# Output columns dealt in turns of 32 to two halves, and three moved operations, in a chain of an FFT filter and two MLPs

## The chip, the cores and the metric

The kernel runs on one core of a Trainium2 chip. TensorE (PE) multiplies matrices, ACT, DVE and POOL work on whole tiles, SP issues most of the transfers, and 16 DMA engines carry them. The metric is the device time of one execution in microseconds (us). Three executions of the kernel before took 1126.7 us in the median (1125.58 to 1127.02).

## The reference

```python
X = np.fft.rfft(x, axis=1)                     # x: 2 x 3008 x 256, fp32
y = np.fft.irfft(X * (filt_r + 1j * filt_i), n=3008, axis=1)
x = y.reshape(6016, 256)
h = x @ w_in                                   # 256 -> 2048
x = (h / (1 + exp(-h))) @ w_out                # 2048 -> 256
g = x @ w_gate                                 # 256 -> 1536
v = x @ w_val
out = (g / (1 + exp(-g)) * v) @ w_out2         # 1536 -> 256, 6016 x 256 fp32
```

## The kernel before

Every matrix product is made from three products of operands split into a high and a low part. The program has an FFT stage (to some 125 us of the span), the first MLP with the preparation of all weights (to some 560 us), and the gated MLP. The change touches the preparation of w_out2 (key `o2`) and the gated MLP.

**The gated MLP.** The 6016 tokens go in six blocks t of 1024 (the last has 896), each of two token halves l. A block has six units (`Pair`, u = 6t + n, u from 0 to 35). A unit makes the gate g and the value v of a slice of the hidden width, by a scheme with seven products of half blocks (`Gate`: p15, p6, p3, p7, p4 and an `add` of product 2). Between its matmuls (`product`, L843) a queue feeds matmuls of the output products (`product7`, L1157): seven products k for each pair c of units, also by halves. In all a unit has 63 matmuls of 128x512, some 14.3 us, of which 21 are output products.

**What sets the order.** `run` (from L1013) writes a unit's steps down in order, with seven calls of `tick()` and calls `side(-1)` to `side(4)` between them. A tick advances the output products by one step: it splits a coming operand into high (`high7`, ACT L1104) and low (`lower7`, DVE L1109), adds finished products into the output tiles (`after7`, DVE L1130, ACT L1132), and issues weights (`load7`, SP L1118, tiles w7 from DRAM tensors d7). A side runs what a table (`later`, L1375 to L1396) puts there: `load_s2` (SP L648, weights wst from ds_g and ds_v for the next unit), x for the next block, and the stores of the block before. Each engine keeps its program's order, and a load can start only after SP has issued all that stands ahead of it.

**The gate's chain in a unit.** ACT computes silu of g.a (L1030) and of g.u2 (L1034). For u2, DVE first adds (L904, in p3). In p7 DVE adds c (L912). The value half starts with a copy of a bank by ACT (L876, `p15`) to which PE adds its products 6 and 7: PE waits for this copy. `join` (DVE L1011) ends the unit before. DVE's L1048 multiplies the value half a into silu of g.a.

**Stores.** Output products are by columns: half m of the 256 output columns, half l of the tokens. The sum for (t, m, l) ends in tile `oa`. `store2` (L1254) transposes one such part by 32x32 squares (DVE L1260) into a tile `ob` of pool tp, and SP sends it with four DMAs (L1265), one for each 32 partitions. They are held in `lag` until the next side. The output rows are 256 columns of fp32 in DRAM, and each DMA writes 32 columns, so its runs are of 128 bytes. For the last block, the last stores go from both SP and ACT at the end (`product8`).

**w_out2's preparation.** `load_w` loads raw weights, `comb_a` (POOL L516, L518) forms sums and differences of four quarters, `pieces` splits them into high (ACT L545, L550) and low (DVE L546 or POOL L551) and `store` sends them to d7 in DRAM.

**Pools.** Tiles of operands come from `mid`; those in the pool `late` (nine buffers: ga, w7, one ho) and `late2` (x and xo of the gated MLP) exist only in the gated MLP. SP's DMAs use eight semaphores in turn.

Of the kernel before, what the change touches and what calls it, by code (L numbers as in the profile page):

```python
# [29 lines left out]
P = 128  # L30
# [89 lines left out]
def fft_filter_mlp_kernel(  # L120
# [307 lines left out]
    def load_w(key, q, half):  # L428


        src = SRC[key]
        raw = mid([P, 512, 2], "raw", U32)
        raws[key, q, half] = raw
        if key == "o2":
            for j in range(2):
                r0 = 512 * q + 256 * half + P * j
                nc.sync.dma_start(
                    raw.rearrange("p (m j c) w -> p j m (c w)", m=2, j=2)[:, j],
                    src[r0:r0 + P, :].rearrange("p (m e) -> p m e", m=2),
                )  # L440
# [69 lines left out]

    def comb_a(key, q, part=None):
        v = pair[key, q] if key == "i1" else pair[key, q].bitcast(F32)
        if part != 1:
            sums[key, q] = mid([P, 4, 256], "ws")
        s = sums[key, q]
        sub = lambda o, a, b: nc.gpsimd.tensor_tensor(o, a, b, op=ALU.subtract)  # L516
        if part != 1:
            nc.gpsimd.tensor_tensor(s[:, 0], v[:, 0, 256:], v[:, 1, 256:], op=ALU.add)  # L518
            sub(s[:, 1], s[:, 0], v[:, 0, :256])
        if part != 0:  # L520
            sub(s[:, 2], v[:, 0, :256], v[:, 0, 256:])
            sub(s[:, 3], v[:, 1, :256], s[:, 1])
            if key == "i1":
                del pair[key, q]
# [14 lines left out]
    def pieces(q, keys, v):  # L539
        w = mid([P, len(keys), 2, 2, P], "wst", F32R)  # L540
        v = v.rearrange("p o (j c) -> p o j c", j=2)
        for n, k in enumerate(keys):
            o = w[:, n]
            if k in MINUS:
                nc.scalar.activation(o[:, :, 0], v[:, n], AF.Copy, scale=-1.0)  # L545
                nc.vector.scalar_tensor_tensor(  # L546
                    o[:, :, 1], v[:, n], -1.0, o[:, :, 0], op0=ALU.mult, op1=ALU.subtract
                )
            else:
                nc.scalar.copy(o[:, :, 0], v[:, n])  # L550
                nc.gpsimd.tensor_tensor(o[:, :, 1], v[:, n], o[:, :, 0], op=ALU.subtract)  # L551
        for n, k in enumerate(keys):
            store(d7[q][:, AT7.index(k)], w[:, n].rearrange("p j l c -> p (j l c)"))

    def comb_7(q, part):
        if part < 2:
            v = pair["o2", q].bitcast(F32)
            if part == 0:
                pieces(q, (1, 2), v[:, :, :256])
            else:  # L560
                pieces(q, (4,), v[:, 1:, 256:])
                if q == 2:
                    pieces(q, (8,), v[:, :1, 256:])
                del pair["o2", q]
        else:
            i = 2 * (part - 2)
            pieces(q, ((5, 6), (7, 3))[part - 2], sums["o2", q][:, i:i + 2])
            if i:
                del sums["o2", q]
# [413 lines left out]
    class Pair:  # L983
# [29 lines left out]
        def run(self, old, side):  # L1013
# [83 lines left out]
    def high7(c, k, p):  # L1097
        if (k, p) == (1, 0):
# [27 lines left out]
    def after7(c, k):  # L1126
# [8 lines left out]
        if (t, m) not in turned and k in (2, 3, 7, 4):  # L1135
            turned[t, m] = mid([P, 2, 512], "oa")
        o = turned[t, m][:, l, :n] if (t, m) in turned else None
# [62 lines left out]
    def product8(p, v, l, m, i):  # L1200
# [10 lines left out]
        if end and i == 2:  # L1211
            store2(t, m, l, (nc.sync, nc.scalar), o)

    def join8(m, l):
        t = NBLK2 - 1
        o = bank(4 + 2 * l + m)[:, :size2(t) // 2]
        nc.vector.tensor_tensor(o, o, turned[t, m][:, l, :o.shape[-1]], op=ALU.add)

    def tick():
# [27 lines left out]
        for r, o in enumerate((-3, 3, 9, 21)):  # L1247
# [6 lines left out]
    def store2(t, m, l, engines=(nc.sync,), src=None):  # L1254

        n = size2(t) // 2
        if src is None:
# [417 lines left out]
```

## Time and profile before

| | |
|---|---|
| median of three executions | 1126.7 us |
| profiled execution, own time | 1127.43 us |
| its span | 1125.7 us |
| PE busy | 1107.8 us, 98% |
| DVE, ACT, POOL busy | 75%, 69%, 35% |
| granted PE clock | 0.999 of full |
| output stores | 80 of 64 KB and 16 of 56 KB |

The span is what the profiler saw between the first and the last instruction of the profiled execution; 1.7 us lie around it. A time "at 745" is counted from the span's start. "Idle before" an instruction is what its engine waited, and the name behind the arrow is who ended the wait.

### The profile page before, as it was taken

How to read it: one execution, taken by the hardware profiler on the slowest of the kernel's cores; microseconds unless marked ns; L12 is line 12 of the kernel's file. 1: busy time of each engine (PE TensorE's matmuls, PEld its weight loads, DVE VectorE, ACT ScalarE, POOL GpSimd, SP SyncE). 2: the span in 40 equal slices, each digit the busy share in tenths (PEclk: the TensorE clock that was granted, in tenths of full speed). 3: DMA queues.
4: the chain of work that ended last, by engine and by line, in shares of the span. 5: the costliest groups of instructions: out<-in, count | busy, mean ns of one | idle time of the engine just before them, and what ended most of it. 6: DMA issues, size and time to landing. Idle time of an engine off the chain costs nothing.

```text
span 1125.7 us, 15425 instructions
## 1 busy us (share of the span) xinstructions
PE 1107.8 (98%) x4999; PEld 912.2 (81%) x4999; DVE 847.4 (75%) x1316; ACT 772.2 (69%) x1459; POOL 391.6 (35%) x369
## 2 busy tenths in 40 slices
PE   9999999999999999999999999999999999999997
PEld 7588888898888888788877778888888888778886
DVE  5888455567587687687665788898888888888877
ACT  5798766667677677666665676776676677677662
POOL 2667836454431362362101322322322322212220
PEclk9999999999999999999999999999999999999999
DMA  9974443435454445443747569898898898798895
GB/s 244 291 238 122 132 143 110 150 113 198 153 175 153 146 168 195 151 174 130 261 131 264 128 151 240 202 232 235 206 219 240 211 227 235 199 214 227 210 233 108
DMA packets 146977, 212.70 MB, mean 189 GB/s; under 512 B 58704, under 2 KB 88016, under 8 KB 146896
## 3 DMA queue, kind: packets, MB, share of 16 engines
q1 hardware_dynamic: 125280, 179.26, 50.0%
q0 software_dynamic: 17456, 31.79, 16.4%
q10 hardware_dynamic: 4160, 0.66, 0.3%
q8 instruction: 40, 0.66, 0.2%
q14 instruction: 41, 0.34, 0.1%
HBM read 138.20 MB, written 42.73 MB: 161 GB/s over the span
## 4 chain that ended last, share of the span: by engine, by line
PE 86%; DVE 6%; ACT 3%; DMA 2%; issue 2%; POOL 0%; SPq 0%; DVEq 0%; ACTq 0%
PE bk L843 25%; PE acc L742 15%; PE bk L1157 11%; PE acc L719 7%; PE h L669 6%; PE y L843 6%; PE xb L843 4%; PE xa L843 4%; PE s L206 2%; PE s L397 2%; PE s L209 2%; DMA wst<-ds_g 1%; PE s L282 1%; ACT ho L1104 1%; DVE ho L1109 1%
## 5 line engine op out<-in xcount | busy, mean ns | idle before, releaser
L742 PE MATMUL acc<-h,w 128*128 128x512 f32 x768 | 283.7, 389 | 0.0
L843 PE MATMUL bk<-xo,wst 128*128 128x512 f32 (+1 forms) x864 | 278.5, 387 | 5.1 <-ACT bk L876 2.9
L1157 PE MATMUL bk<-ho,w 128*128 128x512 f32 (+1 forms) x714 | 264.7, 387 | 0.9 <-DMA w<-d 0.9
L843 PE MATMUL bk<-xo,w 128*128 128x512 f32 (+1 forms) x648 | 208.9, 389 | 2.5 <-DVE c L912 1.9
L843 PEld LDWEIGHTS bk<-xo,wst 128*128 128x128 f32 x864 | 160.9, 188 | 42.1 <-ACT bk L876 7.9
L742 PEld LDWEIGHTS acc<-h,w 128*128 128x128 f32 x768 | 144.2, 188 | 29.6
L1091 POOL DMA_DIRECT2D ga<-c x68 | 59.6, 1100 | 308.6 <-DVE ho L1109 307.7
L1157 PEld LDWEIGHTS bk<-ho,w 128*128 128x128 f32 x714 | 133.9, 188 | 25.5 <-DMA w<-d 1.3
L843 PEld LDWEIGHTS bk<-xo,w 128*128 128x128 f32 x648 | 120.7, 188 | 31.7 <-DVE c L912 7.4
L1109 DVE TENSOR_TENSOR ho<-ga,ho 128x512 fp32r<-128x512 f32 (+1 forms) x136 | 95.2, 707 | 2.2 <-ACT ho L1104 2.2
L719 PE MATMUL acc<-h,w 128*128 128x512 f32 (+1 forms) x384 | 95.4, 376 | 0.0
L1104 ACT CAST ho<-ga 128x512 fp32r<-128x512 f32 (+1 forms) x136 | 82.8, 616 | 3.5 <-PE bk L843 2.7
L669 PE MATMUL h<-xh,w 128*128 128x512 f32 (+1 forms) x248 | 83.6, 379 | 0.1
L719 PEld LDWEIGHTS acc<-h,w 128*128 128x128 f32 x384 | 71.2, 188 | 11.2
L876 ACT COPY bk<-bk 128x512 f32<-128x512 f32 (+1 forms) x72 | 40.6, 565 | 54.2 <-PE bk L843 52.0
L677 DVE TENSOR_TENSOR h<-h,h 128x512 fp32r<-128x512 f32 (+1 forms) x64 | 41.4, 655 | 47.9 <-ACT h L676 46.5
L843 PE MATMUL xb<-xo,wst 128*128 128x512 f32 x192 | 74.7, 391 | 1.6 <-DVE h L939 1.6
L843 PE MATMUL xa<-xo,w 128*128 128x512 f32 x192 | 75.6, 395 | 0.0
L843 PE MATMUL y<-xo,wst 128*128 128x512 f32 x192 | 74.7, 389 | 0.0
L1109 DVE TENSOR_TENSOR ho<-c,ho 128x512 fp32r<-128x512 f32 (+1 forms) x102 | 72.6, 712 | 0.7 <-ACT ho L1104 0.6
L904 DVE TENSOR_TENSOR u<-bk,u 128x512 f32<-128x512 f32 (+1 forms) x72 | 48.7, 677 | 26.5 <-PE bk L843 23.3
L894 ACT COPY u<-bk 128x512 f32<-128x512 f32 (+1 forms) x72 | 41.9, 581 | 32.3 <-PE bk L843 26.9
(166 smaller groups left out, 2190.9 us busy)
## 6 DMA issues: line engine op xcount, KB each, us to landing
w<-d SPq DMA_DIRECT2D x53, 512.0 KB, 5.3
wst<-ds_g SPq DMA_DIRECT2D x36, 512.0 KB, 5.2
wst<-ds_v SPq DMA_DIRECT2D x36, 512.0 KB, 5.7
wst<-ds SPq DMA_DIRECT2D x32, 512.0 KB, 4.5
ga<-c POOLq DMA_DIRECT2D x60, 256.0 KB, 5.7
c<-ga POOLq DMA_DIRECT2D x30, 256.0 KB, 8.5
zt<-d SPq DMA_DIRECT2D x16, 384.0 KB, 5.4
d<-z SPq DMA_DIRECT2D x11, 512.0 KB, 4.3
```

What stands on the lines that cost most here:

```text
L669: nc.tensor.matmul(ps[:, :n], wt[key, f // 4, g][:, wpart, o:o + P], x[xpart][:, g, :n], start=(g == 0 and k == 0), stop=(g == 1 and k == 2),)
L677: nc.vector.tensor_tensor(h[:, 1, :n], u[:, :n], h[:, 0, :n], op=ALU.subtract)
L719: nc.tensor.matmul(a[:, :n], w[:, wpart, o:o + 128], h[:, xpart, :n], start=(f == 0 and k == 0), stop=(f == 15 and k == 2),)
L742: nc.tensor.matmul(a, w[:, wpart, o:o + 128], h[xpart][:, n * l:n * l + n], start=(f == 0 and k == 0), stop=(end and k == 1), skip_group_c ...
L843: nc.tensor.matmul(o, w(wpart), x[:, xpart, :o.shape[-1]], start=(first and k == 0), stop=(last and k == 2), skip_group_check=True,)
L876: nc.scalar.copy(self.y, self.a)
L894: nc.scalar.copy(self.u2, self.y)
L904: nc.vector.tensor_tensor(self.u2, self.b, self.u2, op=ALU.add)
L1091: nc.gpsimd.dma_start(o, v, accum_op=ALU.add)
L1104: nc.scalar.copy(x[:, 0, :v.shape[-1]], v)
L1109: nc.vector.tensor_tensor(x[:, 1, :n], v, x[:, 0, :n], op=ALU.subtract)
L1157: nc.tensor.matmul(o, w7[c, k][:, p, wpart], ops7[c, k, p][:, xpart, :n], start=(k in (1, 5) and p == 0 and i == 0), stop=(k in (2, 3, 4) ...
```

## The change

Output columns were halves 0 to 127 and 128 to 255. Now they are dealt in turns of 32: half m = 0 has columns 0 to 31, 64 to 95 and so on. To that end the quarters of w_out2 are read through strided views with runs of 32 (`turned_in`), in as many instructions as before, and w_out2 is loaded with one DMA for two. Two parts (m = 0 and 1) of one token half are transposed into one tile `ob` where a token's 64 neighbouring columns lie side by side, and four DMAs send it in runs of 256 bytes. So `turned` is keyed by token half, and the table of stores changes: transposes stand at (3,1) and (3,3) for l = 1 and both at (5,0) for l = 0, where there were four places with a group of stores each.

Besides, three operations move: the silu of g.u2 stands behind the next tick and p7 on ACT, DVE's L1048 stands behind its tick, and `load7` for r = 0 is issued one tick later. One more `ho` tile comes from pool `late`. Lines of the changed kernel are some 7 higher here (L1034 is L1043, L876 is L883, L648 is L655, L1118 is L1125), and the stores' 16 (L1265 is L1281).

```diff
 def load_w:  if key == "o2":
-            for j in range(2):
-                r0 = 512 * q + 256 * half + P * j
-                nc.sync.dma_start(...)
+            r0 = 512 * q + 256 * half
+            nc.sync.dma_start(
+                raw.rearrange("p (j f) w -> p j (f w)", j=2),
+                src[r0:r0 + 256, :].rearrange("(j p) f -> p j f", p=P),
+            )
...
+    def turned_in(v):
+        return v.rearrange("p o (x m c) -> p o m x c", m=2, c=32)
...
+        if key == "o2":
+            s, v = s.rearrange("p k (x c) -> p k x c", c=32), turned_in(v)
+            v00, v01, v10, v11 = (v[:, o, m] for o in range(2) for m in range(2))
...
             g.p3()
-            nc.scalar.activation(a[:, n:m], g.u2, AF.Silu)
             tick()
             g.p7()
+            nc.scalar.activation(a[:, n:m], g.u2, AF.Silu)
             side(1)
...
             v.add(v.a, 2, last=True)
+            tick()
             nc.vector.scalar_tensor_tensor(a[:, :n], v.a, -1.0, a[:, :n], op0=ALU.mult, op1=ALU.mult)
-            tick()
             v.p3()
...
-        if (k, p) == (1, 0):
+        if (k, p) in ((1, 0), (2, 0)):
             x = late["p"].tile([P, 2, 512], F32R, tag="mid", name="ho")
...
-        for r, o in enumerate((-3, 3, 9, 21)):
+        for r, o in enumerate((-2, 3, 9, 21)):
...
-    def store2(t, m, l, engines=(nc.sync,), src=None):
+    def store2(t, m, l, src=None, engines=(nc.sync,)):
         n = size2(t) // 2
+        if (t, l) not in outs:
+            if l and t < NBLK2 - 1:
+                outs[t, l] = late2["p"].tile([P, 16, 2, 32], F32, tag="x", name="ob", bufs=5)
+            else:
+                outs[t, l] = mid([P, 16, 2, 32], "ob")
+        o = outs[t, l]
         if src is None:
-            src = turned[t, m][:, l, :n]
-        o = tp.tile([P, 512], F32, tag="u", name="ob")
-        nc.vector.transpose(o[:, :n], src)
+            src = turned[t, l][:, m, :n]
+        nc.vector.transpose(o[:, :n // 32, m], src.rearrange("p (j c) -> p j c", c=32))
+        if m == 0:
+            return
...
-                    out[r0:r0 + n, P * m + 32 * i:P * m + 32 * i + 32].rearrange("(j r) c -> r j c", r=32),
-                    o[32 * i:32 * i + 32, :n].rearrange("p (j c) -> p j c", c=32),
+                    out[r0:r0 + n, 64 * i:64 * i + 64].rearrange("(j r) e -> r j e", r=32),
+                    o[32 * i:32 * i + 32, :n // 32].rearrange("p j m c -> p j (m c)"),
...
-        for n, k, m, l in ((3, 1, 0, 0), (3, 3, 0, 1), (4, 1, 1, 1), (5, 1, 1, 0)):
+        for n, k, m, l in ((3, 1, 0, 1), (3, 3, 1, 1), (5, 0, 0, 0), (5, 0, 1, 0)):
             later(6 * t + n, k, store2, t - 1, m, l)
```

The order on three engines, before and after.

On ACT in unit 3, from the silu of g.a to the copy that PE waits for (CAST is the high part of a coming operand, the first COPY is that of `after7`). Before:

```order
L1030 ACTIVATE ga_5885<-bk_5544 128x512
L1034 ACTIVATE ga_5885<-u2_5874 128x512
L1104 CAST ho_5892<-c_5678 128x512
L1132 COPY bk_5895<-bk_5868 128x512
L1104 CAST ho_5909<-ga_5791 128x512
L1104 CAST ho_5911<-c_5753 128x512
L876 COPY bk_5618<-bk_5543 128x512
```

After:

```order
L1037 ACTIVATE ga_5879<-bk_5538 128x512
L1111 CAST ho_5885<-c_5672 128x512
L1139 COPY bk_5888<-bk_5862 128x512
L1043 ACTIVATE ga_5879<-u2_5868 128x512
L1111 CAST ho_5903<-ga_5785 128x512
L1111 CAST ho_5905<-c_5747 128x512
L883 COPY bk_5612<-bk_5537 128x512
```

One cast and one copy that stood behind the silu of u2 now stand ahead of it.

On DVE at the boundary of blocks 1 and 2 (unit 11), from `join` on. Before:

```order
L1011 TENSOR_TENSOR c_6891<-bk_5543,c_6820 128x512
L1109 TENSOR_TENSOR ho_6915<-c_6352,ho_6915 128x512
L904 TENSOR_TENSOR u2_6925<-bk_5618,u2_6925 128x512
L1109 TENSOR_TENSOR ho_6929<-c_6480,ho_6929 128x512
L912 TENSOR_TENSOR c_6955<-bk_5542,s5_6909 128x512
L1260 STREAM_TRANSPOSE ob_6959<-oa_6187 128x512
```

After:

```order
L1018 TENSOR_TENSOR c_6874<-bk_5537,c_6806 128x512
L1274 STREAM_TRANSPOSE ob_6912<-oa_5998 128x16x32 x2
L1116 TENSOR_TENSOR ho_6898<-c_6346,ho_6898 128x512
L911 TENSOR_TENSOR u2_6909<-bk_5612,u2_6909 128x512
L1116 TENSOR_TENSOR ho_6916<-c_6474,ho_6916 128x512
L919 TENSOR_TENSOR c_6941<-bk_5536,s5_6892 128x512
```

The transpose behind the sum for c is now two transposes, behind `join` and ahead of the sum for u2.

On SP in block 4, from the load ds_g_98 for unit 28 to ds_v_100 for unit 30 (the number after ds_g or ds_v tells the six of a block, 94 to 99 and 100 to 105; w are the w7 tiles). Before:

```order
L648 DMA wst<-ds_g_98 128x1024
L1265 DMA out_dram<-ob 32x16x32 x4
L648 DMA wst<-ds_v_104 128x1024
L1118 DMA w_9165<-d_2_111 128x512
L1265 DMA out_dram<-ob 32x16x32 x4
L1118 DMA w_9207<-d_0_109 128x1024
L1118 DMA w_9242<-d_1_110 128x1024
L648 DMA wst<-ds_g_99 128x1024
L1265 DMA out_dram<-ob 32x16x32 x4
L648 DMA wst<-ds_v_105 128x1024
L1118 DMA w_9359<-d_1_110 128x1024
L648 DMA wst<-ds_g_94 128x1024
```

After:

```order
L655 DMA wst<-ds_g_98 128x1024
L655 DMA wst<-ds_v_104 128x1024
L1125 DMA w_9123<-d_2_111 128x512
L1281 DMA out_dram<-ob 32x16x64 x4
L1125 DMA w_9166<-d_0_109 128x1024
L655 DMA wst<-ds_g_99 128x1024
L1125 DMA w_9215<-d_1_110 128x1024
L655 DMA wst<-ds_v_105 128x1024
L1125 DMA w_9316<-d_1_110 128x1024
L1281 DMA out_dram<-ob 32x16x64 x4
L655 DMA wst<-ds_g_94 128x1024
L655 DMA wst<-ds_v_100 128x1024
```

Between the loads ds_g_98 and ds_g_99 stood two groups of stores and three w7 loads; now there are one group and two w7 loads. The group behind ds_g_99 is gone, and a group stands ahead of ds_g_94, where before one followed it (below the rows shown).

## Rows read from the trace of the kernel before

**Rows 1.** The page, part 1: busy us, share of the span, instructions of each engine.

```profile
PE 1107.8 (98%) x4999; PEld 912.2 (81%) x4999; DVE 847.4 (75%) x1316; ACT 772.2 (69%) x1459; POOL 391.6 (35%) x369
```

**Rows 2.** Busy time by stretch: PE, PEld, DVE, ACT, POOL (instructions), clock, DMA share, GB/s.

```profile
1000.00:1100.00 100.00, 96.98 (x452) 84.03 (x450) 82.71 (x141) 67.80 (x137) 23.65 (x27) 1.00 0.90 221
```

**Rows 3.** Waits of PE: line, releaser, total us, times, longest us.

```profile
PE bk L843 <- ACT bk L876: 2.9, 7, 1.3
PE bk L843 <- DMA wst<-ds_g: 2.1, 2, 1.2
PE bk L843 <- DVE c L912: 1.9, 3, 1.0
PE xb L843 <- DVE h L939: 1.6, 2, 1.0
```

**Rows 4.** PE in order of time: start, length, line, shape, [idle before, releaser].

```profile
632.99 0.84 PE L843 MATMUL bk<-xo,w 128*128 128x512 f32 x3
635.18 0.50 PE L843 MATMUL bk<-xo,wst 128*128 128x512 f32 x1 [1.34 <-ACT bk L876]
...
663.47 0.74 PE L843 MATMUL bk<-xo,wst 128*128 128x512 f32 x2 [0.28 <-ACT bk L876]
...
750.46 0.74 PE L843 MATMUL bk<-xo,wst 128*128 128x512 f32 x2 [0.28 <-ACT bk L876]
...
755.62 0.39 PE L843 MATMUL bk<-xo,wst 128*128 128x512 f32 x1
```

**Rows 5.** ACT in order of time, unit 3 and block boundary at 745 us.

```profile
631.95 0.63 ACT L1034 ACTIVATE ga<-u 128x512 f32<-128x512 f32 x1 [0.88 <-DVE u L904]
...
634.55 0.57 ACT L876 COPY bk<-bk 128x512 f32<-128x512 f32 x1
...
746.71 0.63 ACT L1034 ACTIVATE ga<-u 128x512 f32<-128x512 f32 x1 [1.10 <-DVE u L904]
```

**Rows 6.** DVE in order of time at the same boundary.

```profile
744.62 0.68 DVE L1011 TENSOR_TENSOR c<-bk,c 128x512 f32<-128x512 f32 x1
745.22 0.68 DVE L1109 TENSOR_TENSOR ho<-c,ho 128x512 fp32r<-128x512 f32 x1
745.98 0.69 DVE L904 TENSOR_TENSOR u<-bk,u 128x512 f32<-128x512 f32 x1
```

**Rows 7.** DVE transposes grouped by shape: count, busy us, mean ns, idle before.

```profile
L1260 DVE STREAM_TRANSPOSE ob<-oa 128x512 f32<-128x512 f32 x20 | 14.0, 699 | 0.0
```

**Rows 8.** SP issuing in order of time, five stretches: start, length, line, count.

```profile
748.52 3.67 SPq L1265 DMA_DIRECT2D out_dram<-ob  x4
...
986.61 6.09 SPq L1265 DMA_DIRECT2D out_dram<-ob  x4
...
996.77 0.37 SPq L648 DMA_DIRECT2D wst<-ds_g  x1
...
1098.10 6.04 SPq L1118 DMA_DIRECT2D w<-d  x3
...
1117.45 4.43 SPq L1265 DMA_DIRECT2D out_dram<-ob  x8
```

**Rows 9.** PE in order of time, late: the matmuls behind three waits.

```profile
1004.49 0.47 PE L843 MATMUL bk<-xo,wst 128*128 128x512 f32 x1 [1.17 <-DMA wst<-ds_g]
...
1087.34 0.44 PE L843 MATMUL bk<-xo,wst 128*128 128x448 f32 x1 [0.96 <-DMA wst<-ds_g]
...
1099.17 0.36 PE L1157 MATMUL bk<-ho,w 128*128 128x448 f32 x1
...
1104.67 0.47 PE L1157 MATMUL bk<-ho,w 128*128 128x448 f32 x1 [0.88 <-DMA w<-d]
```

**Rows 10.** Chain of waits, two of its longest pieces: start, us, what.

```profile
996.77 7.58 DMA wst<-ds_g
1080.36 6.85 DMA wst<-ds_g
```

**Rows 11.** Loads of line 648: from issue to landing.

```profile
DMA to landing us min/median/max: 3.1/5.3/8.8
```

More of the change, by code (lines that the diff above doesn't have):

```diff
@@ L515, in comb_a @@
         s = sums[key, q]
+        if key == "o2":
+            s, v = s.rearrange("p k (x c) -> p k x c", c=32), turned_in(v)
+            v00, v01, v10, v11 = (v[:, o, m] for o in range(2) for m in range(2))
+        else:
+            v00, v01, v10, v11 = (v[:, o, m:m + 256] for o in range(2) for m in (0, 256))
         sub = lambda o, a, b: nc.gpsimd.tensor_tensor(o, a, b, op=ALU.subtract)
         if part != 1:
-            nc.gpsimd.tensor_tensor(s[:, 0], v[:, 0, 256:], v[:, 1, 256:], op=ALU.add)
-            sub(s[:, 1], s[:, 0], v[:, 0, :256])
+            nc.gpsimd.tensor_tensor(s[:, 0], v01, v11, op=ALU.add)
+            sub(s[:, 1], s[:, 0], v00)
         if part != 0:
-            sub(s[:, 2], v[:, 0, :256], v[:, 0, 256:])
-            sub(s[:, 3], v[:, 1, :256], s[:, 1])
+            sub(s[:, 2], v00, v01)
+            sub(s[:, 3], v10, s[:, 1])
             if key == "i1":
@@ L540, in pieces @@
         w = mid([P, len(keys), 2, 2, P], "wst", F32R)
-        v = v.rearrange("p o (j c) -> p o j c", j=2)
         for n, k in enumerate(keys):
-            o = w[:, n]
+            x = v[:, n].rearrange("p (j i) c -> p j i c", j=2)
+            h, l = (w[:, n, :, i].rearrange("p j (i c) -> p j i c", c=32) for i in range(2))
             if k in MINUS:
[L545 to L548, printed above, removed]
-            else:
-                nc.scalar.copy(o[:, :, 0], v[:, n])
-                nc.gpsimd.tensor_tensor(o[:, :, 1], v[:, n], o[:, :, 0], op=ALU.subtract)
+                nc.scalar.activation(h, x, AF.Copy, scale=-1.0)
+                nc.vector.scalar_tensor_tensor(l, x, -1.0, h, op0=ALU.mult, op1=ALU.subtract)
+            else:
+                nc.scalar.copy(h, x)
+                nc.gpsimd.tensor_tensor(l, x, h, op=ALU.subtract)
         for n, k in enumerate(keys):
@@ L556, in comb_7 @@
         if part < 2:
-            v = pair["o2", q].bitcast(F32)
+            v = turned_in(pair["o2", q].bitcast(F32))
             if part == 0:
-                pieces(q, (1, 2), v[:, :, :256])
+                pieces(q, (1, 2), v[:, :, 0])
             else:
-                pieces(q, (4,), v[:, 1:, 256:])
+                pieces(q, (4,), v[:, 1:, 1])
                 if q == 2:
-                    pieces(q, (8,), v[:, :1, 256:])
+                    pieces(q, (8,), v[:, :1, 1])
                 del pair["o2", q]
@@ L566, in comb_7 @@
             i = 2 * (part - 2)
-            pieces(q, ((5, 6), (7, 3))[part - 2], sums["o2", q][:, i:i + 2])
+            s = sums["o2", q][:, i:i + 2].rearrange("p k (x c) -> p k x c", c=32)
+            pieces(q, ((5, 6), (7, 3))[part - 2], s)
             if i:
@@ L1134, in after7 @@
         m, l = {2: (0, 0), 3: (0, 1), 6: (0, 1), 7: (1, 1), 5: (1, 1), 4: (1, 0)}[k]
-        if (t, m) not in turned and k in (2, 3, 7, 4):
-            turned[t, m] = mid([P, 2, 512], "oa")
-        o = turned[t, m][:, l, :n] if (t, m) in turned else None
+        if (t, l) not in turned and k in (2, 3, 7, 4):
+            turned[t, l] = mid([P, 2, 512], "oa")
+        o = turned[t, l][:, m, :n] if (t, l) in turned else None
         if k == 5:
@@ L1211, in product8 @@
         if end and i == 2:
[L1212 removed]
+            store2(t, m, l, o, (nc.sync, nc.scalar))
     def join8(m, l):
@@ L1216, in join8 @@
         o = bank(4 + 2 * l + m)[:, :size2(t) // 2]
-        nc.vector.tensor_tensor(o, o, turned[t, m][:, l, :o.shape[-1]], op=ALU.add)
+        nc.vector.tensor_tensor(o, o, turned[t, l][:, m, :o.shape[-1]], op=ALU.add)
     def tick():
@@ L1252, in fft_filter_mlp_kernel @@
     turned = {}
-    def store2(t, m, l, engines=(nc.sync,), src=None):
+    outs = {}
+    def store2(t, m, l, src=None, engines=(nc.sync,)):
         n = size2(t) // 2
+        if (t, l) not in outs:
+            if l and t < NBLK2 - 1:
+                outs[t, l] = late2["p"].tile([P, 16, 2, 32], F32, tag="x", name="ob", bufs=5)
+            else:
+                outs[t, l] = mid([P, 16, 2, 32], "ob")
+        o = outs[t, l]
         if src is None:
-            src = turned[t, m][:, l, :n]
-        o = tp.tile([P, 512], F32, tag="u", name="ob")
-        nc.vector.transpose(o[:, :n], src)
+            src = turned[t, l][:, m, :n]
+        nc.vector.transpose(o[:, :n // 32, m], src.rearrange("p (j c) -> p j c", c=32))
+        if m == 0:
+            return
         r0 = STEP2 * t + n * l
```

4 lines of the change are left out of this document (removed).

## The prediction

> **What bounds the kernel now.** I read the busy times first. TensorE (PE) is busy 1107.8 of a span of 1125.7 us [rows 1], so all that any edit around it can win is the rest, some 18 us. The table of stretches comes next: late in the gated MLP PE stands at 96.98 of 100 us, at full granted clock, with the DMA engines at a share of 0.90 [rows 2]. Third, PE's waits by releaser say who takes the time [rows 3]: ACT's bank copy 2.9 us in seven waits, the gate weights' load 2.1 in two, DVE's combining add 1.9 in three, and 1.6 in two in stage 1. Last, the order of time around each wait. A matmul lasts 0.39 but the next one starts 0.23 after it (three take 0.84 [rows 4]), and idle time is counted from the modelled end; so a wait shown as x has cost x + 0.16.
>
> The program order on PE does not change, nor its operands' shapes. The change can act only through those waits, through new ones, and through the end.
>
> **The silu moved on ACT.** In unit 3, the silu of u2 (L1034) stands idle for 0.88 until DVE's add, starts at 631.95, and the copy of L876 that PE waits for starts at 634.55, five ACT operations later [rows 5], so 0.52 each. The wait is 1.34, cost 1.50 [rows 4]. After the change, a cast and a bank copy stand ahead of the silu, where the idle time was, and three instead of five steps lie between. The two need 1.04 and find 0.88, so the silu starts 0.16 later and the copy 1.04 - 0.16 = 0.9 earlier: **-0.9**. If those two are not ready so early, it is 0.
>
> Six more waits of this kind make up the other 1.56 of the 2.9. One is at 663.47 (0.28, cost 0.44 [rows 4]), at the first block boundary, where no stores fall due; one is in unit 27, built like unit 3, near 983; if the other five are like 663.47 it is 1.56 - 5 x 0.28 = 0.16, and costs 0.32 or a little more. Each is shorter than 0.9 and goes: with 0.1 each for the weight load that follows a wait late, **-1.0** for the two. The other four are at later boundaries, as 750.46 [rows 4]. There the silu starts at 746.71, 1.10 after ACT was free, since it waits for L904 on DVE [rows 5]. That add starts at 745.98; the join and the subtraction ahead of it start at 744.62 and 745.22, 0.60 apart [rows 6], so DVE has 745.98 - 745.82 = 0.16 to spare. Now two transposes stand between join and add; they last 0.70 [rows 7] where the others last 0.68 [rows 6], so 0.60 each on the queue, and the add starts 1.2 - 0.16 = 1.04 later. Behind it two ACT steps fewer give back 1.04: sum **0**. At these four the DVE add for c (L912) is 1.0 later as well; I take 0 for it, up to +0.2 each.
>
> The other moved operation (L1048, now behind its tick on DVE) lets the tick's subtraction go first; its own result is wanted several operations later, so 0.
>
> **Stores on SP.** Output goes from 20 groups of four stores to 10 in the run, each group with as many runs (2048) of twice the bytes. The group at 986.61 holds SP for 6.09; with the load that follows, the gate load due after it is issued only at 996.77 [rows 8]. It is 7.58 on its way [rows 10], and PE waits 1.17 [rows 9]. The same pattern ends at 1087.34 with 0.96 [rows 9], behind a load issued at 1080.36 and 6.85 on its way [rows 10]. Now one group of the two is left ahead of this load, and the second of the w7 loads, which waits for its buffer, stands behind it. Were that group as slow and over as late, at 986.61 + 6.09 = 992.7, and the one w7 load left as long as 2, the gate load would go at 994.7, 2 us earlier than 996.77, more than either wait. Cost was 1.17 + 0.16 and 0.96 + 0.16, **-2.5**; bounds 0 and -2.7.
>
> The Trainium skill speaks against this term ("DMA: Bandwidth & Descriptors", section "Issuing engines are not separate DMA queues"): DMAs of all issuers share the same 16 engines, and the time on the issuing sequencer is "usually small relative to the DMA itself". By that the load is late because the engines are full, and the term would be near 0. The 6.09 for four issues [rows 8] is nearly as long as the load's 7.58 [rows 10], so here it is not small; yet it may be long for the very reason that the engines were full.
>
> **What the stores now stand ahead of.** At the four later boundaries both transposes are done at 744.62 + 0.68 + 2 x 0.6 + 0.1 = 746.6, four stores follow, and only then the load ds_g0 of the next unit, which was ahead of the stores before. PE first uses it at 755.62 [rows 4]. The group took 3.67 here, behind that load [rows 8]; without it I take 3.0: issue at 749.6, plus the median of 5.3 [rows 11] gives 754.9, 0.7 in time. With 6.09 [rows 8] and 8.8 [rows 11] it is 761.5, 5.9 late. The margin is thin; I take 0.2 a boundary, **+0.8**, bounds 0 and +23.
>
> **The last w7 loads.** Late in the program the load that PE waits for at 1104.67 (0.88) [rows 9] is issued at 1098.10 [rows 8]. Its buffer is now another one, free only with the matmul of 1099.17 [rows 9], 16 before its use: issue some 1.5 later. The stores ahead of it are earlier by about 2, so its way should be shorter than the 6.5 that lie between 1098.10 and PE's start. I take **+0.2**, bounds -1.0 (the wait goes) and +1.5 (the same way).
>
> **Stage 1.** POOL, ACT and DVE read w_out2's combinations in runs of 32 instead of 256, in unchanged counts; no row shows such an access. POOL is busy 35% [rows 1], and these steps reach PE only where a piece delays DVE's subtraction: 1.6 in two waits [rows 3]. One more such wait is +0.8, a lucky shift -0.3. I take **+0.2**, nearer to nothing. Six fewer loads at SP there are hidden.
>
> **The end.** Eight stores on SP take 4.43, 0.55 each [rows 8]; the last group has two of them on SP and two on ACT, before and after. Before, the group of the transpose just ahead still held the queue; now nothing does, but each store carries twice the bytes: **-0.2**, bounds -0.6 and +0.6.
>
> **Sum.** -0.9 - 1.0 - 2.5 + 0.8 + 0.2 + 0.2 - 0.2 = -3.4. The profiled execution took 1127.43, so 1124.0; the median of the runs, 1126.7, is 0.7 below it, so **1123.3** there.
>
> **Rivals.** 1. The loads were late because the engines were full; the 2.5 stays, and the smaller terms leave -0.9: 1125.8. For it: a share of 0.90 [rows 2]. The Trainium skill's rule above points the same way. Against: half the packets of the stores go.
> 2. Slower: ds_g0 behind the stores. From the first store to the load's landing it has 755.6 - 746.6 = 9.0 us. At 3.67 + 8.8 = 12.5 it is 3.5 late, four times 14.0: 1126.7 - 3.4 - 0.8 + 14.0 = 1136.5. It makes the kernel slower by 2.2 once that time passes 9.0 + (2.2 + 4.2) / 4 = 10.6. For it: a group followed by a load is what was slow at 986.61. Against: at these places SP stood free before, and medians give 8.3.
> 3. More goes than I count. With fewer packets, loads and POOL's additive DMAs land earlier, the 1.9 behind L912 [rows 3] and 1104.67's 0.88 go (with 0.16 and 0.1 each, 3.8), and ds_g0 costs nothing (0.8): about 1118.5.
>
> **How the numbers follow.** Forecast 0.50, with a range of its own from 1121.5 to 1125.3; rival 1 0.24; rival 2 0.11; rival 3 0.13; anything else 0.02. A measurement of this kernel tells 0.2%, 2.25 us, from no change: faster means below 1124.4, slower above 1129.0. Of the forecast's half about 0.42 lies below 1124.4 and the rest within; with rival 3 and a little of rival 1 faster has 0.60, within 0.29, slower 0.11. The range from 1118.3 to 1128.5 leaves out most of rival 2 and the far end of rival 3.
>
> **What would show it.** Right: no PE wait on a gate load near 1003 and 1086, the wait of unit 3 down to some 0.4, that of 663 gone, the four at boundaries unchanged, SP's store groups halved in number. Wrong: a PE wait on ds_g at the first use in units 12, 18, 24 and 30 (rival 2); gate loads in the last two blocks still over 7 us on their way with PE waiting (rival 1); transposes well over 0.70, or new waits on DVE at the boundaries; new waits in stage 1 on L939.

## The result, and the profile after

The changed kernel took 1143.7 us in the median of six executions (1138.3 to 1148.3), the kernel before 1126.6 beside it: a ratio of 1.015, with an interval of 1.0123 to 1.0177. I had forecast 1123.3. The profiled execution has a span of 1140.1 and took 1141.9 in all; before it was 1125.7 and 1127.4. So the two spans differ by 14.4, and the rows below say where they do.

PE's waits by releaser in the changed kernel (as [rows 3] of before):

```profile
PE bk L850 <- DMA wst<-ds_g: 9.2, 4, 2.9
PE bk L850 <- ACT bk L883: 5.6, 6, 2.5
PE bk L850 <- DVE c L919: 3.2, 5, 1.0
PE xb L850 <- DVE h L946: 1.6, 2, 1.0
...
PE bk L1164 <- ACT oa L1156: 0.7, 1, 0.7
```

The waits on the gate load, 2.1 in two, are 9.2 in four. These four are new. The two of before, near 1003 and 1086 [rows 9], are gone, and so is the one on a w7 load. The waits on ACT's copy are fewer and longer, and those on the sum for c are five.

The chain of waits has the four loads among its longest pieces (start, us, what), against two others before [rows 10]:

```profile
749.52 7.05 DMA wst<-ds_g
841.51 6.17 DMA wst<-ds_g
930.47 7.60 DMA wst<-ds_g
1022.88 7.17 DMA wst<-ds_g
```

They are ds_g0 at the four block boundaries that have stores. SP in order of time at the first, and then PE (idle before in brackets):

```profile
744.61 4.81 SPq L1281 DMA_DIRECT2D out_dram<-ob  x4
749.52 1.37 SPq L655 DMA_DIRECT2D wst<-ds_g  x1
```

```profile
754.12 0.39 PE L850 MATMUL bk<-xo,w 128*128 128x512 f32 x1
756.71 0.47 PE L850 MATMUL bk<-xo,wst 128*128 128x512 f32 x1 [2.21 <-DMA wst<-ds_g]
...
757.95 1.27 PE L850 MATMUL bk<-xo,w 128*128 128x512 f32 x3
...
761.15 0.60 PE L1164 MATMUL bk<-ho,w 128*128 128x512 f32 x1
761.58 0.65 PE L850 MATMUL bk<-xo,w 128*128 128x512 f32 x2
```

Two things are to be seen. The group of stores begins when I had said (2 us after `join`), but holds SP for 4.81 instead of 3.0; the load behind it takes 7.05 instead of 5.3, and lands 11.96 after the first store. PE waits 2.21. Then, from 757.95 on, matmuls start 0.43 apart instead of 0.23: PE runs at half speed for some eight matmuls. The table of stretches shows that as the granted clock (last three columns: clock, DMA share, GB/s), where [rows 2] had 1.00:

```profile
750.00:760.00 10.00, 7.79 (x31) 6.05 (x30) 7.28 (x13) 4.91 (x10) 2.12 (x3) 0.91 1.05 253
...
840.00:850.00 10.00, 7.70 (x33) 5.90 (x33) 8.34 (x15) 5.94 (x12) 2.63 (x3) 1.00 1.06 242
...
935.00:945.00 10.00, 7.51 (x27) 5.73 (x26) 7.08 (x12) 4.15 (x8) 0.00 (x0) 0.83 0.88 275
```

The level is full (2.4 GHz) on either side and half (1.2) for a few us behind three of the four waits, and behind one of 2.47 in the last block. Behind the shortest of the five, 1.6 near 847, it stays full. In all, 32 matmuls run slow: 23 behind those three waits and 9 behind the one in the last block.

The wait in the last block is ACT's. PE's row, and ACT's in the same place:

```profile
1108.89 0.67 PE L850 MATMUL bk<-xo,wst 128*128 128x448 f32 x2 [2.47 <-ACT bk L883]
```

```profile
1106.45 0.56 ACT L1111 CAST ho<-c 128x448 fp32r<-128x448 f32 x1 [4.05 <-PE bk L1164]
...
1108.31 0.52 ACT L883 COPY bk<-bk 128x448 f32<-128x448 f32 x1
```

ACT stands 4.05 idle before this cast of a coming operand, until PE has read the tile that the cast is to overwrite. PE meanwhile wants the copy L883, which is queued behind the cast.

Last, DVE and POOL in a unit with n = 3, where PE waits for the sum for c (L919):

```profile
713.08 3.08 DVE L1116 TENSOR_TENSOR ho<-c,ho 128x512 fp32r<-128x512 f32 x1
```

```profile
713.38 2.22 POOL L819 TENSOR_TENSOR s<-x,x 128x512 f32<-128x512 f32 x1
```

The subtraction takes 3.08 instead of 0.68 and ends 0.56 after POOL's addition. Three of these units (blocks 1 to 3) are new in this; the one in block 4 had it before, at 976.94 with 2.96.

What I had hoped for came as well. The wait of unit 3, 1.34 in [rows 4], is 0.35:

```profile
633.74 0.50 PE L850 MATMUL bk<-xo,wst 128*128 128x512 f32 x1 [0.35 <-ACT bk L883]
```

The waits at 663 and in unit 27 are gone. The end takes 10.8 from the start of the last 24 matmuls, where it took 10.95, and stage 1 has two waits of 1.6 in all on DVE's L946, as before.

The account is counted after 560 us from one matmul's start to the next, against 0.227 (0.198 for 448 columns). By it PE loses 15.0 more than before. Waits on gate loads went from 2.4 to 9.8 (+7.4), matmuls at half clock from nothing to 5.9 (4.6 behind the three boundary waits, 1.3 in the last block), waits on the copy from 4.0 to 6.5 (+2.5), those on the sum for c from 2.3 to 4.0 (+1.6); +0.8 on L1156, -1.0 for the w7 load, and -2.2 in many small ones make the 15.0.

### The profile page after: what moved, and what is told of

Read it like the earlier page. It is cut to its first block, busy times and chain, and to the rows that moved or that the text cites. A ratio compares the mean times of both kernels' runs of the same rounds, so it can differ in the third digit from the quotient of the medians.

```text
span 1140.1 us, 15274 instructions
## 1 busy us (share of the span) xinstructions
PE 1111.1 (97%) x4999; PEld 917.2 (80%) x4999; DVE 855.1 (75%) x1316; ACT 773.4 (68%) x1459; POOL 391.0 (34%) x369
## 4 chain that ended last, share of the span: by engine, by line
PE 86%; DVE 5%; ACT 3%; DMA 3%; issue 2%; POOL 0%; SPq 0%; DVEq 0%; ACTq 0%
PE bk L850 24%; PE acc L749 15%; PE bk L1164 12%; PE acc L726 7%; PE h L676 6%; PE y L850 6%; PE xb L850 4%; PE xa L850 4%; DMA wst<-ds_g 2%; PE s L206 2%; PE s L397 2%; PE s L209 2%; DVE ho L1116 1%; PE s L282 1%; ACT ho L1111 1%
## 5 line engine op out<-in xcount | busy, mean ns | idle before, releaser
L850 PEld LDWEIGHTS bk<-xo,wst 128*128 128x128 f32 x864 | 163.5, 190 | 51.3 <-ACT bk L883 8.3
L1116 DVE TENSOR_TENSOR ho<-ga,ho 128x512 fp32r<-128x512 f32 (+1 forms) x136 | 92.1, 684 | 26.1 <-ACT ho L1111 26.1
L1116 DVE TENSOR_TENSOR ho<-c,ho 128x512 fp32r<-128x512 f32 (+1 forms) x102 | 80.8, 792 | 3.2 <-ACT ho L1111 3.2
L883 ACT COPY bk<-bk 128x512 f32<-128x512 f32 (+1 forms) x72 | 40.7, 566 | 59.7 <-PE bk L850 54.3
L1111 ACT CAST ho<-c 128x512 fp32r<-128x512 f32 (+1 forms) x102 | 62.5, 613 | 10.8 <-PE bk L1164 10.8
```

The costliest lines, as they stand in the source:

```text
L850: nc.tensor.matmul(o, w(wpart), x[:, xpart, :o.shape[-1]], start=(first and k == 0), stop=(last and k == 2), skip_group_check=True,)
L883: nc.scalar.copy(self.y, self.a)
L1111: nc.scalar.copy(x[:, 0, :v.shape[-1]], v)
L1116: nc.vector.tensor_tensor(x[:, 1, :n], v, x[:, 0, :n], op=ALU.subtract)
```

## The experiments

**Theory A**: the four stores ahead of ds_g0 make that load late, and the clock falls behind the longer waits. **Theory B**: the new `ho` tile in the small pool makes ACT wait for PE, and the rest follows. **Theory C**: the doubled runs load the DMA engines, in whatever order. Theory D, on DVE and POOL, came beside them.

**1. Stores one side later.** Changed kernel, with

```diff
-            lag.append(send)
+            lag.append((lambda: lag.append(send)) if l == 0 else send)
```

> The changed kernel with one edit: at the block boundary the four stores are sent one side later, so that the gate load ds_g0 stands ahead of them on SP, as it did before. Theory A (the load behind the stores is late, and PE's clock falls after the long waits): the four waits on ds_g (9.2 us shown) go, and with them the matmuls at half speed behind three of them (some 4 us); 1143.7 - 13 = about 1130, slower than before by the rest. Theory B (the ho tile taken from the small pool makes ACT wait for PE): the waits on ds_g are a consequence of ACT's; the time stays within 3 us of 1143.7. Theory C (stores with twice the bytes hold the DMA engines, whatever the order): the loads at the boundary are still late by over 1 us each, the time falls by under 6 us.

Measured: 1129.55, a ratio to the kernel before of 1.0023 (1.0014 to 1.0032). SP at the first boundary, in order of time, and PE's waits:

```profile
745.17 0.32 SPq L655 DMA_DIRECT2D wst<-ds_g  x1
745.58 5.25 SPq L1281 DMA_DIRECT2D out_dram<-ob  x4
```

```profile
PE bk L850 <- ACT bk L883: 5.5, 6, 2.5
PE bk L850 <- DVE c L919: 3.2, 5, 1.0
```

The load goes first, the stores behind it hold SP for 5.25, and no wait on ds_g is left; nor is a matmul slow behind the boundaries. 14.1 of the 17.1 us are this (1143.7 to 1129.55). Theory A holds, with its number of about 1130. Theory B would have left the time within 3 us of 1143.7, and theory C the loads late; neither is so.

**2. The ho tile back in pool mid.** Changed kernel, with

```diff
-        if (k, p) in ((1, 0), (2, 0)):
+        if (k, p) == (1, 0):
```

> The changed kernel with one edit: the ho tile of (k=2, p=0) comes from pool mid again. Theory A: the four waits on ds_g stay near 9 us; only ACT's waits of 1.68 (four times) and 4.05 before that cast go, which cost PE 2.6 in the last block and some 0.4 at each boundary, and the clock's fall behind the wait of 2.47: 4 to 6 us less, 1138 to 1140. Theory B: most of the 17 us goes, below 1131.

Measured: 1139.0 (1133.6 to 1144.1, four executions), ratio 1.0106 (1.0074 to 1.0139). The wait in the last block goes, and in its place PE waits for a w7 load there:

```profile
PE bk L850 <- DMA wst<-ds_g: 7.3, 3, 3.0
PE bk L850 <- DVE xo L809: 3.3, 1, 3.3
...
PE bk L1164 <- DMA w<-d: 2.6, 1, 2.6
```

One of the four boundaries shows its wait as 3.3 on DVE's xo here; the other three are on ds_g. The profiled execution is the longest of the four (1144.1), so its sum is not that of the median. By the median the tile is worth 4.7, as theory A had it, but with four executions so far apart the interval (1.0074 to 1.0139) overlaps that of the changed kernel (1.0123 to 1.0177). The late loads stay. So do the copy's waits of 0.68 at the four boundaries, which I had expected to go with the tile.

**3. The order alone, in the kernel before.** Stores of (m=1, l=0) ahead of ds_g0, in runs of 128 bytes:

```diff
-((3, 1, 0, 0), (3, 3, 0, 1), (4, 1, 1, 1), (5, 1, 1, 0))
+((3, 1, 0, 0), (3, 3, 0, 1), (4, 1, 1, 1), (5, 0, 1, 0))
```

> The kernel before with one edit: the transpose and the stores of (m=1, l=0) stand one tick earlier, so that a group of four stores in runs of 128 bytes (256 KB in all) stands ahead of ds_g0 at the four boundaries. Theory A (order on SP alone): the load is issued about 4 us later and is late by 1 to 3 us four times, with a fall of the clock behind the longer ones: 1132 to 1142. Theory C (the runs of 256 bytes and the 512 KB of a group are what makes it late): no wait over 0.5 us, 1126 to 1128.5.

Measured: 1128.5, ratio 1.0013 (1.0004 to 1.0022). SP at the first boundary:

```profile
745.31 4.01 SPq L1265 DMA_DIRECT2D out_dram<-ob  x4
749.36 1.26 SPq L648 DMA_DIRECT2D wst<-ds_g  x1
```

That is not what theory A said (1132 to 1142); it lies in theory C's range (1126 to 1128.5), by which the runs of 256 bytes and the 512 KB of a group make the load late. A group of 256 KB ahead of the load, with as many runs, holds SP for 4.01 here, 4.0 to 5.0 at the four boundaries. The load lands 9.3 to 10.2 after the first store, where it is 11.4 to 12.6 in the changed kernel. Of the difference, 0.3 to 0.9 is that the load is issued sooner, and 1.2 to 2.3 that its way is shorter (5.0 to 5.5 for 6.2 to 7.6). No boundary shows a wait on a load, though at the fourth it lands only 0.13 before PE's start. New are longer waits on the copy: the transpose stands ahead of the sum for u2 now and makes three of them 0.70 instead of 0.28 and the fourth 0.57 instead of 0.22, 1.6 in all. That these are the 1.6 us of the median is not shown, since in the profiled execution (1127.0) one wait on a gate load of before is gone as well. So order alone does not do it. It takes the group's size too.

**4. Half the group.** Changed kernel; of the boundary's four stores (and of the same token half's group in the last block) only two are sent, so half of those tokens' columns are left out.

```diff
-            for i in range(4):
+            for i in range(2 if l == 0 and t < NBLK2 - 1 else 4):
```

> The changed kernel, which sends only two of the four stores of a boundary's group (half of the columns of those tokens are left out): 256 KB in 1024 runs of 256 bytes ahead of ds_g0. If it is the amount ahead of the load that counts (SP held for about half of 4.8 us, and half the packets ahead), the load lands some 3 us earlier: the waits on ds_g go or are under 0.5, and the clock does not fall there, 1129 to 1132. If it is the position behind any store at all, the load is still late by over 1 us at each boundary, over 1136.

Measured: 1129.0, ratio 1.0018 (1.0009 to 1.0026), all four waits gone. SP at the first boundary:

```profile
745.00 0.97 SPq L1281 DMA_DIRECT2D out_dram<-ob  x2
746.07 1.78 SPq L655 DMA_DIRECT2D wst<-ds_g  x1
```

The load goes out 1.07 after the first store instead of 4.91, and though it is 7.8 on its way it is in time. So it is the amount ahead of the load. Here it acts through the issue time alone (1.0 to 1.8 for 4.7 to 5.4, while the way grows by 0.3 to 1.2); between experiment 3 and the changed kernel it acts more through the load's way.

**5. The gate operations alone, in the kernel before.**

```diff
             g.p3()
-            nc.scalar.activation(a[:, n:m], g.u2, AF.Silu)
             tick()
             g.p7()
+            nc.scalar.activation(a[:, n:m], g.u2, AF.Silu)
...
+            tick()
             nc.vector.scalar_tensor_tensor(a[:, :n], v.a, -1.0, ...)
-            tick()
```

> The kernel before with the two moved gate operations alone (silu of u2 behind the next tick and p7 on ACT, L1048 behind its tick on DVE). As the prediction had it: the wait of unit 3 falls from 1.34 to about 0.4, the one at 663 goes, at the later boundaries two ACT steps are won since the transposes are not moved here, 4 x 0.4: together -2.5 to -4, 1122.5 to 1124. Rival D (DVE, now earlier, meets POOL's additions of x in units n=3 and one subtraction takes 3 us instead of 0.7, as at 713 of the changed kernel): four new waits of 0.6 on the sum for c take 2 to 3 us back, 1125.5 to 1127.

Measured: 1122.1, ratio 0.9951 (0.9938 to 0.9965). All waits on the copy but one go (0.4 is left of 2.9). Rival D's new waits in units n = 3 don't appear; the one of before, 0.75 at 982, is 0.35 here:

```profile
PE bk L843 <- DMA wst<-ds_g: 2.0, 1, 2.0
...
PE bk L843 <- ACT bk L876: 0.4, 1, 0.4
```

So the gate order is worth 4.8, a little more than the 2.5 to 4 expected and more than the prediction's 1.9, since without moved transposes it also clears the boundaries; 3.5 of it are waits on the copy, counted from start to start.

**6. Store groups away from ds_g5.** The kernel of 5, with two groups of stores later:

```diff
-((3, 1, 0, 0), (3, 3, 0, 1), (4, 1, 1, 1), (5, 1, 1, 0))
+((3, 1, 0, 0), (4, 1, 0, 1), (4, 3, 1, 1), (5, 1, 1, 0))
```

> The kernel before with the two moved gate operations, and two of its store groups two and three sides later, (4,1) and (4,3) for (3,3) and (4,1), so that only loads stand between ds_g4's stores and the load ds_g5. Theory of the prediction's term of -2.5 (ds_g5 is late because SP is held by store groups ahead of it): the wait on ds_g of 2.0 near 1080 goes, 1120.0 to 1120.8 against 1122.1. Rival 1 of the prediction (the engines are full): it stays over 1 us, 1121.5 to 1122.5.

Measured: 1120.35, ratio 0.9951 (0.9939 to 0.9963), by the ratio no more than the run without this edit. The wait on ds_g is gone, and on a w7 load it is 1.7 where it was 0.7:

```profile
PE bk L1157 <- DMA w<-d: 1.7, 1, 1.7
```

The wait went, as this theory had it, but not for its reason. The load ds_g5 of block 4 is issued at the same time in both kernels, whose `join` stands at 985.64 and 985.62. First the run of 5, then this one:

```profile
991.53 0.37 SPq L648 DMA_DIRECT2D wst<-ds_g  x1
```

```profile
991.47 0.38 SPq L648 DMA_DIRECT2D wst<-ds_g  x1
```

In both, SP came to it when PE (L1157) had freed the buffer of the w7 load ahead, and not when it was done with stores. What changed is the load's way, 7.53 in the one and 4.72 in the other; a block later it is 7.96 and 4.73, issued 5.3 behind `join` in both. So the stores ahead, with the w7 load behind them (issued at 988.19 in the one and 981.77 in the other), made the way long and not the issue late. The DMA share of 0.92 from 1000 to 1100 in both runs is a mean over 100 us and does not show this.

Moving the last group too, to (5, 3), so that one w7 load stands ahead of it, was meant to remove the 1.7 on a w7 load:

> The kernel before with the two moved gate operations and the store groups at (3,1), (4,1), (4,3) and (5,3): as the run at 1120.35, and the boundary's group also behind ds_v0 and, at the end, behind one w7 load. If the wait of 1.7 on a w7 load in the last block comes from the stores ahead of it, it goes: 1118.3 to 1119.3. If the load is late for its buffer alone, 1120 to 1121.

Measured: 1120.5, ratio 0.9945 (0.9933 to 0.9958), and the waits on w7 loads in its profiled execution (1123.9, the longest) are 3.5 in two. The stores now stand ahead of the next w7 load: the wait moved and did not go. The time is in the range for that outcome (1120 to 1121).

**7. Both edits of 1 and 2.**

> The changed kernel with both edits: stores at the boundary sent one side later, and the ho tile of (k=2, p=0) from pool mid. Theory A (the two causes add): from 1129.5 the wait of 2.47 in the last block and some 0.4 at four boundaries go, 1125 to 1126. Rival (the pool mid has no room for this tile: in the run with the tile alone a wait of 2.6 on a w7 load came in the last block): that wait comes back and takes the gain, 1128 to 1130.

Measured: 1127.3, ratio 1.0008 (0.9999 to 1.0018), between the two ranges. The rival was nearer: the wait in the last block went, and one of 2.2 on a w7 load came. What was left were the four copies at boundaries and the sums for c. With POOL's additions for x one side later as well (`later(u + 3, 2, prep_x2, t, 0)`):

> As the kernel with both edits, and POOL's three additions for the next block's x (L819) stand one side later in units n=3, so that DVE's subtraction (L1116, 3.08 us at 713 of the changed kernel instead of 0.68) no longer starts just ahead of them. Theory D (the long subtraction comes from POOL's additions beside it): the four waits on the sum for c (0.62 shown three times, 0.35 once) go, 2 to 3 us less than without this edit, and no subtraction over 2 us is left. Rival (it comes from POOL's DMA issues ahead of it): the waits stay and the time is the same within 1 us.

Measured: 1126.5, ratio 1.0005 (0.9996 to 1.0015). No subtraction takes over 2 us and the waits in units n = 3 go, but waits of 0.40 on the same sum come near 727, 815 and 903, where additions and subtractions meet anew (1.6 to 1.8 for one). That is 0.8 less in the median, within the spread, where 2 to 3 were expected. So the waits went as theory D has it, and the long subtraction does come from POOL's additions beside it; the time stayed as its rival has it, since part of the gain was given back at the new places.

**8. load7 back.** As 7, and `enumerate((-3, 3, 9, 21))` again:

> The changed kernel with the boundary's stores one side later, the ho tile from pool mid, and load7 for r=0 one tick earlier, as before: what is left of the change's order is both transposes at (5,0). Theory (the move of load7 takes a wait off POOL, whose additions then start 0.24 us earlier and stretch DVE's subtraction to 3.08): against 1127.3 with load7 later, the four waits on the sum for c (0.6 shown three times, 0.36) go, and the late w7 load's wait of 2.2 is smaller, together 3 to 5 us: 1122.5 to 1124.5; the four waits of 0.69 at the boundaries stay and are what separates it from 1119.3. Rival (the transposes' place moves POOL against DVE): the waits on the sum for c stay, 1126 to 1127.5.

Measured: 1125.75, ratio 0.9991 (0.9982 to 1.0001). The waits on the sum for c fall from 3.4 to 1.5, those in units n = 3 of blocks 1 to 3 are gone; the late w7 load is 2.5 late all the same:

```profile
PE bk L850 <- ACT bk L883: 3.1, 5, 0.7
PE bk L1164 <- DMA w<-d: 2.5, 1, 2.5
...
PE bk L850 <- DVE c L919: 1.5, 3, 0.9
```

The time, 1.6 below that of 7 with intervals that touch, lies in neither range: the waits of units n = 3 behave as the theory has it, the w7 load does not. So in these two kernels load7's place decides whether POOL meets DVE. But not alone: the small pool's tile and load7's move put into the kernel before show no new wait on the sum for c.

```diff
-        if (k, p) == (1, 0):
+        if (k, p) in ((1, 0), (2, 0)):
...
-        for r, o in enumerate((-3, 3, 9, 21)):
+        for r, o in enumerate((-2, 3, 9, 21)):
```

> The kernel before with two edits alone: the ho tile of (k=2, p=0) from the small pool and load7 for r=0 one tick later. Theory (these two, not the stores, bring ACT's wait for PE in the last block and the stretched subtractions): a wait of 2 to 3 us on the copy L876 in the last block, longer waits on L876 at the boundaries, four waits of some 0.6 on the sum for c in units n=3: 1130 to 1135. Rival (they need the moved gate operations or the moved transposes to show): 1126 to 1128.

Measured: 1127.6, ratio 1.0006 (0.9997 to 1.0015). ACT in the last block, in order of time, where the cast waits 2.6 by the profile for a load into the tile:

```profile
1093.25 0.56 ACT L1104 CAST ho<-c 128x448 fp32r<-128x448 f32 x1 [2.62 <-DMA w<-d]
```

The wait in the last block is here, 2.0 on PE, and it comes from these two edits. It is paid for by the gate and w7 loads that are now in time, so that the kernel stays where it was, as the rival has it. The rest of the theory failed: neither the boundaries nor the sums for c changed. The gate loads came in time here with the store groups as before: the w7 load that SP waited with now stands behind ds_g5, which is issued 4.1 behind `join` in block 4 instead of 5.9 and is 5.0 on its way instead of 7.6.

**9. Transposes behind the sum, stores behind both loads.** The changed kernel, with the tile and load7 as before, and

```diff
-((3, 1, 0, 1), (3, 3, 1, 1), (5, 0, 0, 0), (5, 0, 1, 0))
+((3, 1, 0, 1), (3, 3, 1, 1), (5, 1, 0, 0), (5, 3, 1, 0))
```

> The changed kernel with the boundary's two transposes at (5,1) and (5,3) instead of both at (5,0), so behind the sum for u2, and with their stores behind both loads ds_g0 and ds_v0; the ho tile of (k=2, p=0) comes from pool mid and load7 for r=0 is one tick earlier, as before. Theory (three causes add: position of the stores, the two transposes ahead of the sum for u2 with 0.69 shown and 0.85 lost at each of four boundaries, and the pool's ho tile): against 1127.3 of the kernel with the first and third alone, the four waits on the copy L883 go (-3.4) and the late w7 load's wait falls from 2.2 towards 0.9 (-1.3, and the slowed matmuls behind it -1.2): 1121.5 to 1124. Rival (the doubled runs cost elsewhere, in loads behind the group): new waits on w7 or ds of 1 to 3 us, 1125 to 1128.

Measured: 1119.3 (1118.5 to 1120.2), ratio 0.9931 (0.9918 to 0.9943): faster than both kernels, and than the 1121.5 to 1124 expected. PE's waits:

```profile
PE bk L850 <- DVE c L919: 1.5, 3, 0.9
PE bk L1164 <- DMA w<-d: 1.3, 1, 1.3
...
PE bk L850 <- ACT bk L883: 0.4, 1, 0.4
```

The same with the small pool's tile and the later load7 kept:

> The same transposes and stores as in the run with them last, but the ho tile of (k=2, p=0) stays in the small pool and load7 stays one tick later, as in the changed kernel. Theory (that tile's cast waits for PE's last use of a w7 tile, while PE waits for a copy queued behind the cast on ACT): the wait of some 2.5 on L883 in the last block is there, whatever the stores do, and the boundaries' waits are small: 1.5 to 3 us over the run without it, 1124 to 1126. Rival (it came from the transposes that stood ahead): it is gone, the same time as that run within 1 us.

Measured: 1127.5, ratio 1.0006 (0.9997 to 1.0015). The two settings are worth 8.2 here, more than the 1.5 to 3 expected for the tile's wait: the 2.5 on the copy, 2.7 on a w7 load with slow matmuls behind it, and three sums for c:

```profile
PE bk L850 <- DVE c L919: 3.4, 6, 1.0
PE bk L850 <- ACT bk L883: 2.8, 2, 2.5
PE bk L1164 <- DMA w<-d: 2.7, 1, 2.7
```

POOL's and DVE's rows of these two kernels, in the same unit, differ by a quarter of a us. First the run at 1119.3, where `join` starts at 713.22, then the one at 1127.5, where it starts at 712.88:

```profile
713.81 0.68 DVE L1116 TENSOR_TENSOR ho<-c,ho 128x512 fp32r<-128x512 f32 x1
```

```profile
714.35 2.00 POOL L819 TENSOR_TENSOR s<-x,x 128x512 f32<-128x512 f32 x1
```

```profile
713.48 3.08 DVE L1116 TENSOR_TENSOR ho<-c,ho 128x512 fp32r<-128x512 f32 x1
```

```profile
713.77 2.22 POOL L819 TENSOR_TENSOR s<-x,x 128x512 f32<-128x512 f32 x1
```

An addition that begins 0.54 behind the subtraction's start leaves it at 0.68; one that begins 0.29 behind it makes it 3.08. Why POOL gets there earlier is in its own order of time: a wait of 0.36 between its first two DMA issues is there in the one and not in the other. The first kernels of 7 and 8, which differ in load7 alone, show the same pair: with load7 as before the wait, and an addition 1.13 behind `join`; with load7 later no wait, and 0.90. Why load7's place makes that wait stays open.

## Why the prediction was wrong

The step that failed is the one on **what the stores now stand ahead of**, put at +0.8. It measured 14.1, the difference to the kernel with the load first. Its rule was right, and its rival was named: it goes by the time from the first store to the load's landing, and past 10.6 us the kernel is slower by over 2.2. That time is 11.4 to 12.6 at the four boundaries. Three sizes were off. First, the group's issue was taken as 3.0, since the load ahead of it would be gone; it is 4.6 to 5.3, and 5.25 with the load back ahead of it. I let the bytes double and the issue time shrink, though a row gave 3.67 at this very place and 6.09 as the top. Second, the way of the load was taken as the median over all loads, 5.3, where loads right behind a group were the ones to look at; it is 6.2 to 7.6. Third, I took a late PE to cost what it waits. The clock adds some 4.6 us behind three of the four waits, which no rival had; so the 14.0 that I priced for the rival at 3.5 late was reached at 2.5.

The forecast was 20.4 below the result, and this step is 13.3 of it. By the account, most of the rest is the small pool's tile with load7's move, some 5, and the four boundaries' copies, 1.7.

Point by point:

- Silu moved: right. The wait of unit 3 fell by 0.99 (0.9 forecast), 663's and unit 27's went. Alone the two gate operations give 4.8.
- The four boundaries, "sum 0": wrong, 0.41 to 0.44 more lost at each. The sum for u2 is later as I said, but it is not what holds ACT. The cast ahead of the silu of g.a waits 1.68 for PE there:

```profile
744.46 0.62 ACT L1111 CAST ho<-c 128x512 fp32r<-128x512 f32 x1 [1.68 <-PE bk L1164]
...
746.50 0.62 ACT L1043 ACTIVATE ga<-u 128x512 f32<-128x512 f32 x1
...
748.58 0.58 ACT L883 COPY bk<-bk 128x512 f32<-128x512 f32 x1
```

  The first kernel of 8, without the small pool's tile, has the same 1.68; the kernel of 9, which takes the tile `ob` from `mid` a tick later, has it no more, nor has that of 3, whose `ob` comes from tp. So I put it down to the tile taken earlier and what it leaves to the next cast, which I had not followed; no run changes the pool of `ob` alone, so this is argued and not shown.
- The small pool's tile and load7's move: costed as one w7 load, +0.2. That load was in time after all; the wait moved to ACT's cast (2.47, and slow matmuls behind it), and three waits of 0.6 on sums for c came.
- ds_g5, -2.5: right in the amount, both waits are gone, and right in the step that the load is issued sooner: 2.5 and 2.0 behind `join` instead of 5.9 and 5.3. I had laid this on two things, one group of stores fewer ahead and the w7 load that now stands behind. Only the second is borne out. Experiment 6 shows the load issued no sooner without the groups, since SP waited for the w7 buffer; the last run of 8, with the groups as before, shows it issued sooner. What the groups' move shortens is the load's way, which I had not counted: 5.0 and 5.6 in the changed kernel instead of 7.6 and 6.9. Either the stores' move or load7's (with the tile) clears both waits without the other (experiments 9 and 8). So rival 1 falls in its time, since the 2.5 did not stay; but the way, on which it laid the delay, is what the stores change.
- Rival 1's sentence from the Trainium skill ("DMA: Bandwidth & Descriptors", section "Issuing engines are not separate DMA queues") has the issue time as usually small beside the DMA itself. For these two loads the trace does not speak against it. At the boundaries it does: four stores took 4.81 to issue and 5.3 to 6.1 each to land, and experiment 4 shows that a shorter issue is enough to bring the load in time.
- The end, -0.2: 0.15. Stage 1, +0.2: 0. POOL's subtractions of w_out2's pieces take 742 ns in the mean with the new views and took 743.

What stays open: why the group of 512 KB holds SP for 4.6 to 5.3 where one of 256 KB with as many runs takes 4.0 to 5.0, and why the load behind it is longer on its way; and which wait lowers the clock. One of 1.6 left it and one of 2.2 did not, but a wait of 2.0 left it in experiment 5 and lowered it in the last run of experiment 8, and the wait of 2.47 in the last block lowered it in the changed kernel and not in that of experiment 1.

## What to carry to other kernels

When stores move ahead of a load, take the group's issue time and the load's way from the slowest rows in which a load stands behind such a group, not from medians, and compare their sum with the slack; if it is close, move the load first, as experiment 1 did. A wait of some 2 us of a busy PE can cost far more than itself, since the clock may fall behind it: the 2.21 of the first boundary cost 4.0 in all. When a load is late, read its issue and its way apart before saying what held it; in experiment 6 the expected cause, a queue held by stores, was not what changed. And a tile taken earlier, or from a smaller pool, is a wait for whoever gets the next one: look whose last read it waits for, and whether that reader waits for something queued behind.

## What the runs showed of the hardware

- Four stores of 128 KB in 512 runs of 256 bytes each took SP 4.6 to 5.3 us to issue at the boundaries; four of 64 KB in 512 runs of 128 bytes 2.7 to 3.8 behind the gate load and 4.0 to 5.0 ahead of it; two of the larger ones 0.9 to 1.7.
- In the changed kernel the granted clock went to half for seven to nine matmuls behind waits of 2.2 to 2.9 us, each matmul 0.2 us longer; behind a wait of 2.47 in the run of experiment 1 it stayed full.
- A gate load of 512 KB issued at the same place was 7.5 to 8.0 us on its way with a group of four stores ahead and 4.7 with that group moved away (experiments 5 and 6).
- A DVE subtraction of 128x512 took 3.08 instead of 0.68 when a POOL addition began 0.3 us behind its start, and 0.68 when it began 0.5 behind it. The Trainium skill ("SBUF — State Buffer", section "SBUF: two separate sides") says that the two engines share a pair of ports as an exclusive lock, which whoever starts first holds for its whole instruction; a DVE operation with two SBUF inputs takes it only against a POOL operation that reads SBUF. The stretched subtraction ends 0.56 after the addition, as a lock would have it; but it began first by the profile, so on who holds it the trace does not agree.
- POOL's 128x256 subtractions took the same on views with runs of 32 elements as on runs of 128.
